# A second V row tile for the recurrent forward, and the next segment's tail rows issued behind the copies of V rows on GpSimd

## Chip, cores, metric

One core of one Trainium2 chip. The metric is device microseconds of a whole execution (forward and all gradients), median of the executions of one kernel. With one core there are no two dies to compare; all profiled runs below are marked fast (granted clock 0.961 to 0.982 over the span).

## The reference, cut to what matters

The program computes a conditioned transformer block and its gradients. The change touches the forward of part A, a recurrence over 64 segments of 32 rows, with 8 memory rows handed on from each segment to the next (32 heads of 128):

```python
mem = mem0
for s in range(n_seg):                     # 64
    h = concatenate([mem, x[:, s*32:(s+1)*32]], axis=1)   # 40 rows
    q, k, v = h @ Wq, h @ Wk, h @ Wv
    p = softmax(where(mask, q @ k.T * scale, -1e9))
    o = (p @ v) @ Wo
    mem = o[:, :8]                          # the next segment needs these
    outs.append(o[:, 8:])
```

## The kernel before

Rows of a segment are split. The first 32 of its 40 rows (8 memory rows and 24 of x) are projected in the segment itself. The last 8 ("tail rows") of four segments are projected together ahead of time into RB. `Vst` holds V by head: rows 0 to 95 are copied from `RA["v"]` on GpSimd (`Vst<-RA0v`), the tail rows 96 to 119 come by six small transfers from `RBv`, issued by GpSimd (`v_tails`). Two transposing transfers on the SyncE queue write V and the exponentials transposed (`VTr<-Vst`, `Pst<-ET`) for the backward. GpSimd scales `Pst` in the next segment (`norm`).

```python
Vst = ptiles("Vst", 1)[0]                       # one tile
...
def v_tails(s):
    rb, o = RBv[(s // nseg_t) % 2], 8 * (s % nseg_t)
    for j in range(3):
        nc.gpsimd.dma_start(Vst[96 + 8*j:104 + 8*j, 0:1024], rb[32*j + o:32*j + o + 8, 0:1024])
        nc.gpsimd.dma_start(Vst[96 + 8*j:104 + 8*j, 1024:1408], rb[96 + o:104 + o, 384*j:384*j + 384])
...
for s in range(NS):                             # one segment
    if norms: norms.pop()()                     # scaling of Pst of segment s-1, then its stores (SyncE)
    proj("k", 0, "dve"); proj("k", 1, "act")    # K rows; half 1 also issues the row store
    if 1 <= s4 <= 3:                            # s4 = s % 4
        p1(s // nseg_t + P1_AHEAD, s4)          # a layernorm step on VectorE: statistics, scale, shift
    proj("q", 0, "dve"); proj("q", 1, "act")
    proj("v", 0, "dve")
    nc.gpsimd.tensor_copy(Vst[0:96, 0:512], RA["v"][0:96, 0:512])       # L776
    turns()                                     # K and Q to heads
    proj("v", 1, "dve")
    nc.gpsimd.tensor_copy(Vst[0:96, 512:1024], RA["v"][0:96, 512:1024]) # L779
    st_exp(0); st_exp(1); vshift(); st_exp(2)
    nc.sync.dma_start(VTr[:], Vst[:, :], transpose=True)                # L793
    den(0); or0 = pv(0)                         # L733: product with Vst
    nc.sync.dma_start(Pst[:], ET[:, :], transpose=True)                 # L798
    ...                                         # pv(1), pv(2), Ost, OT
    at_ps = outproj()
    evac_turned()
    v_tails(s + 1)                              # overwrites Vst: waits for L793's transfer
    tails_in("kq", s + 1)                       # K and Q tails, eight GpSimd copies
    parts = self.split_pair(sb2, at_ps, "at")
    tail.collect(s4, [OT])
    ...                                         # memory rows to the next segment's hT
    self.store_rows(psp, sb2, ft, self.AOA[s], "at", "p")
    if s4 == nseg_t - 1:
        tail.begin(s - nseg_t + 1, [Wo])
    def norm(...):
        nc.gpsimd.tensor_tensor(Pst[0:120], Pst[0:120], rden..., op=mult)   # L851, 2.53 us
        nc.sync.dma_start(self.VT[s], VTr[:])
        nc.sync.dma_start(self.PS[s], Pst[:])                               # L854
    norms.append(norm)
```

All instructions are pinned to program order within their engine. So an instruction that waits holds up everything behind it on that engine: in the segment shown in the prediction L653 waited 4.12 us, to 873.22, and the copies of K and Q tails, which stand behind the six issues and do not need the transpose, started at 876.24.

The softmax here doesn't subtract the row's maximum and nothing guards it: scores larger than these inputs give would overflow.

## Time and profile before

| | before |
|---|---|
| time, median | 3292.5 us (3288.9 to 3294.4, 4 runs) |
| profiled span | 3281.5 us (a run of 3283.3 us, not one of these four) |
| forward: first K product of segment 0 to that of segment 63 | 34.1 to 1083.6 us |
| mean segment (62, the first left out) | 16.45 us |
| TensorE idle in 50 to 1100 us | 89 us |
| windows of 3.41 us at half clock, 100 to 1000 us | 20 |

The lines behind this stand in the prediction. Three things to read from them: which idle time of TensorE is large, what GpSimd does right before that wait ends, and what the next transpose on the SyncE queue had to wait for. The half-clock windows (stretches in which TensorE was granted 0.5 of its clock) are counted from the trace's records of the granted clock, their total time divided by 3.41 us, the length of the shortest of them there.

### The profile page before, as it was taken

What the parts mean: (1) busy time and instruction counts of PE and PEld (TensorE: products, weight loads), DVE (VectorE), ACT (ScalarE), POOL (GpSimd) and SP (SyncE); (2) the same over time, 40 slices, a digit from 0 to 9 for tenths busy, and PEclk for the clock granted to TensorE, in tenths of its full rate; (3) what the DMA queues carried; (4) which work ended last, traced back from release to release, by engine and by line L of the source; (5) the groups of instructions that cost most, each with busy time, mean ns of one, the idle gap of its engine ahead of it and who ended that gap; (6) DMA issues with size and microseconds to landing.
All of it is one profiled execution on the core that took longest, in us unless ns stands there. A gap on an engine that the chain in (4) does not pass through costs nothing.

```text
span 3281.5 us, 98764 instructions
## 1 busy us (share of the span) xinstructions
PE 3020.3 (92%) x40069; PEld 1756.2 (54%) x40069; DVE 1550.0 (47%) x3769; ACT 1160.6 (35%) x2829; POOL 1478.0 (45%) x2973
## 2 busy tenths in 40 slices
PE   5999998999899799997989999999999978999999
PEld 3565655656565444444545555555555543455454
DVE  4555555555555577753235455455555530332321
ACT  2444444444444333322124444444444420110111
POOL 3566665566555366641134444444444430332321
PEclk8999999999999799999999999999999999999999
DMA  8777877777777689887669999999999999998886
GB/s 291 186 186 188 194 190 178 194 187 191 181 185 186 206 208 220 217 231 244 223 169 273 259 259 262 265 262 266 272 263 259 263 235 218 247 213 191 199 231 159
DMA packets 958892, 726.12 MB, mean 221 GB/s; under 512 B 656018, under 2 KB 831138, under 8 KB 958308
## 3 DMA queue, kind: packets, MB, share of 16 engines
q1 hardware_dynamic: 827940, 508.77, 67.9%
q0 software_dynamic: 59056, 148.62, 13.4%
q10 hardware_dynamic: 71440, 62.40, 7.5%
q8 instruction: 316, 5.18, 0.7%
q14 instruction: 140, 1.15, 0.1%
HBM read 294.91 MB, written 276.33 MB: 174 GB/s over the span
## 4 chain that ended last, share of the span: by engine, by line
PE 39%; DMA 8%; issue 5%; ACT 2%; POOL 1%; DVE 1%; SPq 1%; ACTq 0%; POOLq 0%; DVEq 0%
PE dh_ps L212 9%; PE gps L1812 5%; PE pass_ps L249 4%; PE g_ps L1501 3%; PE gps5o L1825 3%; PE gps L1210 3%; PE dh_tps L212 2%; DMA rows<-DKR 2%; PE tps L1416 2%; DMA rows<-OSR 1%; PE dp_ps L1480 1%; PE dp_ps L1488 1%; ACT RAd L61 1%; PE dh_ft L318 1%; PE turn_ps L1382 1%
## 5 line engine op out<-in xcount | busy, mean ns | idle before, releaser
L1812 PE MATMUL gps<-rows,hrows 128*128 128x512 bf16 (+2 forms) x2160 | 417.6, 355 | 1.7 <-ACT ot L61 1.7
L1812 PEld LDWEIGHTS <-hrows 128*128 128x128 bf16 x2160 | 211.3, 98 | 206.3 <-issue 2.1
L249 PEld LDWEIGHTS <-hT 128*32 128x32 bf16 x6144 | 158.0, 97 | 161.4 <-issue 1.8
L1530 POOL COPY dOst<-RAd 96x512 bf16<-96x512 bf16 x128 | 78.5, 614 | 349.5 <-DVE RAd L63 339.4
L653 POOL DMA_DIRECT2D Vst<-RBv x192 | 97.8, 509 | 210.9 <-PE pass_ps L249 122.9
L1816 POOL DMA_DIRECT2D out_dram<-ot x108 | 81.5, 755 | 238.4 <-DVE ot L63 134.3
L63 DVE CAST ot<-gps 128x512 bf16<-128x512 f32 (+3 forms) x76 | 47.9, 633 | 259.2 <-PE gps L1812 142.8
L309 DVE TENSOR_TENSOR dh_lo<-dh_ps,dh_hi 128x256 bf16<-128x256 f32 x128 | 48.4, 420 | 239.1 <-ACT dh_hi L305 239.1
L851 POOL TENSOR_TENSOR Pst<-Pst,rden 120x1408 bf16<-120x1408 bf16 x63 | 159.4, 2530 | 0.0
L1825 PE MATMUL gps5o<-WoT,rows 128*128 128x512 bf16 x600 | 133.2, 384 | 24.1 <-DMA rows<-OSR 24.1
L61 ACT ACTIVATE ot<-gps 128x512 bf16<-128x512 f32 (+3 forms) x75 | 41.1, 548 | 291.8 <-PE gps L1812 139.0
L220 PE MATMUL at_ps<-Wo,OT 128*32 128x256 bf16 x4096 | 138.7, 294 | 0.4
L212 PE MATMUL dh_ps<-WvT,dVT 128*32 128x512 bf16 x2048 | 134.0, 380 | 0.0
L249 PE MATMUL pass_ps<-Wv,hT 128*32 128x512 bf16 x2048 | 133.3, 380 | 0.0
L63 DVE CAST RA0v<-pass_ps 128x512 bf16<-128x512 f32 x128 | 88.5, 692 | 88.9 <-PE pass_ps L249 62.0
L733 PE MATMUL or_ps<-Vst,ET 128*128 128x128 bf16 x704 | 71.7, 228 | 62.9 <-POOL Vst L776 56.6
L1490 DVE SCALAR_TENSOR_TENSOR dS<-dp_ps,Pst_l 128x512 bf16<-128x512 f32 (+1 forms) x192 | 112.2, 640 | 36.6 <-PE dp_ps L1488 36.5
L249 PE MATMUL pass_ps<-WoT,dyT 128*32 128x512 bf16 x2048 | 121.9, 380 | 5.2 <-ACT dyT L1589 5.2
L249 PE MATMUL pass_ps<-Wk,hT 128*32 128x512 bf16 x2048 | 122.8, 382 | 1.5 <-ACT hT L841 1.1
L212 PE MATMUL dh_ps<-WqT,dQT 128*32 128x512 bf16 x2048 | 122.3, 379 | 0.0
L212 PE MATMUL dh_ps<-WkT,dKT 128*32 128x512 bf16 x2048 | 122.3, 380 | 0.0
L61 ACT ACTIVATE dVT<-g_ps 128x512 bf16<-128x512 f32 (+1 forms) x192 | 107.8, 561 | 40.6 <-PE g_ps L1501 22.3
(407 smaller groups left out, 7104.7 us busy)
## 6 DMA issues: line engine op xcount, KB each, us to landing
OSR<-Ost SPq DMA_DIRECT2D x64, 352.0 KB
OT<-OT SPq DMA_DIRECT2D x64, 352.0 KB
VT<-VTr SPq DMA_DIRECT2D x64, 352.0 KB
PS<-Pst SPq DMA_DIRECT2D x64, 352.0 KB
OT_l<-OT SPq DMA_DIRECT2D x64, 352.0 KB
Pst_l<-PS SPq DMA_DIRECT2D x64, 352.0 KB
VT_l<-VT SPq DMA_DIRECT2D x64, 352.0 KB
DKR<-rows_x POOLq DMA_DIRECT2D x64, 352.0 KB, 5.8
```

The costliest lines, as they stand in the source:

```text
L61: return nc.scalar.activation(out, in_, AF.Copy)
L63: return nc.vector.tensor_copy(out, in_)
L212: self.nc.tensor.matmul(ps[32 * j:32 * j + 32, :], lhsT=lhsT, rhs=w, start=(n < 4), stop=(n >= total - 4), tile_position=(0, 32 * j))
L220: nc.tensor.matmul(ps[32 * j:32 * j + 32, :], lhsT=x[k], rhs=w[k][:, 256 * d:256 * d + 256], start=(n == 0), stop=(n == total - 1), tile_p ...
L249: self.nc.tensor.matmul(ps[32 * j:32 * j + 32, :], lhsT=lhs(c), rhs=rhs, start=(c == 0), stop=(c == DC - 1), tile_position=(0, 32 * j))
L653: nc.gpsimd.dma_start(Vst[96 + 8 * j:104 + 8 * j, 0:1024], rb[32 * j + o:32 * j + o + 8, 0:1024])
L851: nc.gpsimd.tensor_tensor(Pst[0:120, :, :], Pst[0:120, :, :], rden[:, :].unsqueeze(2).to_broadcast([120, G, 128]), op=ALU.mult)
L1210: nc.tensor.matmul(ps[:], lhsT=h2r[:, j, c * 128:(c + 1) * 128], rhs=xr[:, j, :], start=(j == 0), stop=(j == NT - 1))
L1490: nc.vector.scalar_tensor_tensor(out=part3(dS, pi), in0=ps[:, 0:n, :], scalar=cfg.scale, in1=part3(Pst, pi), op0=ALU.mult, op1=ALU.mult)
L1501: nc.tensor.matmul(ps[:, j, :], lhsT=lh[:, g * GW:(g + 1) * GW], rhs=rh[:, g * GW:(g + 1) * GW], start=True, stop=True)
L1812: nc.tensor.matmul(ps[:, 0:ng * E], lhsT=hrows[:, tp_, c * 128:(c + 1) * 128], rhs=rows[:, tp_, 0:ng * E], start=(tp_ == 0), stop=(tp_ == ...
L1825: nc.tensor.matmul(pss[gg][:], lhsT=rows[:, tp_, gg * E:(gg + 1) * E], rhs=dyrows[:, tp_, :], start=(tp_ == order[0]), stop=(tp_ == order[ ...
```

## The change

The intent: the tail rows of the next segment go into the other of two V tiles, so they need not wait for the transpose of the present one; and they are issued where GpSimd has nothing to do.

```diff
-            Vst = ptiles("Vst", 1)[0]
+            Vsts = ptiles("Vst", 2)
@@ def v_tails(s)
-                rb, o = RBv[(s // nseg_t) % 2], 8 * (s % nseg_t)
+                Vst, rb, o = Vsts[s % 2], RBv[(s // nseg_t) % 2], 8 * (s % nseg_t)
@@ for s in range(NS)
-                QT, KT = XT["q"], XT["k"]
+                QT, KT, Vst = XT["q"], XT["k"], Vsts[s % 2]
@@ behind the copies L776, L779
                     v_tails(0)
+                if s + 1 < NS:
+                    v_tails(s + 1)
@@ behind outproj(), evac_turned()
                 if s + 1 < NS:
-                    v_tails(s + 1)
                     tails_in("kq", s + 1)
```

## The prediction

> **What bounds the kernel now.** I read, in this order: the page's busy shares, a table of busy time by stretch, the list of waits in the forward stretch (50 to 1100 us), the timelines of TensorE, GpSimd and the SyncE queue over some segments, and the granted clock of single segments. The forward runs 64 segments one after the other, each needing the 8 memory rows of the one before.
>
> The stretch table says that TensorE is busy for 961 of the forward's 1050 us, so all its idle time there is 89 us. Columns: length, then busy us of TensorE, its weight loads, VectorE, ScalarE, GpSimd, then granted clock and DMA share.
>
> ```profile
> 50.00:1100.00 1050.00, 961.08 (x17827) 625.23 (x17828) 557.91 (x1482) 471.11 (x1277) 627.82 (x1341) 0.96 0.75 186
> ```
>
> The waits of that stretch (waiter, what ended the wait, us in total, times, longest):
>
> ```profile
> POOL Vst L653 <- PE pass_ps L249: 122.9, 34, 10.6
> ...
> PE or_ps L733 <- POOL Vst L776: 56.6, 43, 2.8
> ...
> POOL Vst L653 <- DMA VTr<-Vst: 53.9, 18, 4.5
> ...
> PE st_ps L690 <- POOL qT L65: 7.0, 4, 2.3
> ```
>
> Two thirds of TensorE's idle time are one wait: the first product with V (or_ps, L733) waits for GpSimd's copy of V rows into Vst (L776) in 43 of 64 segments. GpSimd in turn sits idle ahead of the tail-row issues (L653), 3.3 us a segment (210.9 us over 64). Most of these waits are put down to a TensorE product long done; the instruction's other wait is the transposing DMA that reads Vst, and I take it to be that one nearly everywhere. One stalled segment on GpSimd, as its timeline has it:
>
> ```profile
> 873.22 0.53 POOL L653 DMA_DIRECT2D Vst<-RBv  x1 [4.12 <-PE pass_ps L249]
> ...
> 875.74 0.51 POOL L654 DMA_DIRECT2D Vst<-RBv  x1
> 876.24 0.76 POOL L65 COPY kT<-b_colsk 128x192 bf16<-128x192 bf16 x4
> 876.95 0.77 POOL L65 COPY qT<-b_colsq 128x192 bf16<-128x192 bf16 x4
> 877.67 0.40 POOL L1886 COPY ao_tail<-OT 128x264 bf16<-128x264 bf16 x1
> 878.02 0.26 POOL L539 COPY hT<-hx 128x96 bf16<-128x96 bf16 x1
> 878.25 2.53 POOL L851 TENSOR_TENSOR Pst<-Pst,rden 120x1408 bf16<-120x1408 bf16 x1
> 880.74 0.60 POOL L776 COPY Vst<-RA0v 96x512 bf16<-96x512 bf16 x1
> 881.29 0.60 POOL L779 COPY Vst<-RA0v 96x512 bf16<-96x512 bf16 x1
> ```
>
> and on the SyncE queue in the same time:
>
> ```profile
> 866.74 1.39 SPq L793 DMA_TRANSPOSE VTr<-Vst  x1
> 868.23 2.04 SPq L798 DMA_TRANSPOSE Pst<-ET  x1
> ...
> 880.81 0.33 SPq L854 DMA_DIRECT2D PS<-Pst  x1
> ...
> 883.60 1.53 SPq L793 DMA_TRANSPOSE VTr<-Vst  x1
> ```
>
> The reader should see a ring. The transpose of Vst is issued at 866.74. The tail rows overwrite the only Vst, so their issue waits for it until 873.22 (6.5 us). Six issues (3.0), eight copies of K and Q tails (1.4), two small copies (0.6) follow in program order, then the scaling of Pst at 878.25 (2.53). The V copy and the store of Pst come behind it (880.74, 880.81); four more issues of the same queue end and the next transpose leaves at 883.60. Round the ring: 16.86 us. From the traces' instruction times over all segments the usual round is 10.8 (transpose issue to scaling) + 2.5 + about 3.1 = 16.4 us. The forward's mean segment is 16.45 (62 segments after the first in 1020 us). So the ring paces most segments, not TensorE alone.
>
> What TensorE needs without stalls is in its timeline: the first Wk products of three consecutive segments start at 582.25, 597.14 and 611.89, so 14.89 and 14.75 us. Sixteen segments with extra conditioning products take 0.66 more.
>
> The stalls cost a second time, through the clock. Columns as above:
>
> ```profile
> 856.50:871.20 14.70, 14.36 (x280) 9.21 (x276) 9.09 (x25) 7.02 (x19) 9.54 (x21) 1.00 0.72 170
> 871.20:889.40 18.20, 16.10 (x291) 10.33 (x287) 9.45 (x24) 7.51 (x20) 9.27 (x20) 0.91 0.76 179
> ```
>
> The second is the segment shown, with 1.98 us of stall; its period is 3.5 us longer than the one before, and TensorE's own busy time is 1.7 us longer at a granted clock of 0.91. The clock records hold about 25 windows of 3.41 us at half clock between 121 and 1100 us.
>
> [...] 0.50 us in the timeline, 3.8 us median to landing for Vst<-RBv. So the six issues are 3.0 us of GpSimd's own time, and moving them doesn't shorten them. [...]
>
> **The change part by part.**
> Removed: the wait of the tail rows for the transpose of the same segment. They now write the other Vst, whose transpose was issued a whole segment earlier and lands around the start of this one; the new place, behind L779, is about 8 us into the segment. I expect no wait there.
> Added: one memset of 0.65 us at the start, and six issues more in segment 0; nothing per segment. The build order shows 2529 GpSimd rows both before and after.
> Moved: 3.0 us of issues, from between the transpose and the scaling to behind the V copies, where GpSimd sat idle for some 3 us until the memory rows (AOA) were ready. That hides them.
>
> The new ring: K and Q tails, collection and hT copy (2.0 us) no longer stand behind the transpose, and run right after AOA near the end of the segment. The scaling then waits for its own input only, the transposed Pst. That one leaves 1.6 us after Vst's. The queue's own waits give its landing where they were still open:
>
> ```profile
> SPq L854 <- DMA Pst<-ET: 12.9, 22, 0.9
> ```
>
> In the rows with a real wait these end 6.0 to 8.0 us after Vst's transpose was issued, usually 7.2. So the ring becomes 7.2 + 2.5 + 3.1 = 12.8 us, 3.6 less than now and about 1.9 below TensorE's 14.75. TensorE should then be the bound: with a transpose issued 9 us into a segment, Pst lands at 16.2, 1.4 into the next; scaling ends at 4.0, before the V rows arrive (5.4), and the V copies finish well ahead of the product at 8.0.
>
> The sum: 62 segments at 14.76 make 915 us, plus 16 x 0.66 = 11, so 926 against 1020: at most 94 us. About 64 of it are direct stalls (56.6 and 7.0); the rest is mostly half-clock time, 25 windows with up to 1.7 us lost in each, partly in the forward's first segments. Not all goes: I leave 8 us for late transposes where the queue also stores the tail K and Q rows (3.8 us of issues in half the segments), [...]and for a few half-clock windows. Gain 86 us, all from the forward; everything behind it is untouched. 3294 - 86 = 3208 us.
>
> **The rivals.**
> First: the landing of Pst takes the place of the removed wait and stays late. Scaling must stand ahead of the V copy in program order, so a late Pst stalls TensorE just as before. For it: [...]DMA share is already 0.75 and rises by a tenth when segments shorten. Against it: landing 6 to 8 us after issue leaves 1 to 2.7 us of slack. If it were true half of the time, the gain would be 40 to 55 us, time 3240 to 3254.
> Second: only the direct wait goes, the half-clock windows stay, since they also come in segments with small stalls. Then the gain is 60 us and the time 3234. Against it: the segments without stall that I checked run at 1.00.
> Third: the SyncE queue becomes the bound, as its stores of tail rows and the four row stores stand ahead of the next transpose. It would hold segments near 15.3 in half of the cases: gain some 75, time 3219.
> Fourth: nothing gained, because the six issues now delay AOA and the K and Q tails. These come at 12 us with two to three to spare, so I give this little.
>
> **Range and chances.** 2% is 3228, a gain of 66. The main line and the third rival are beyond it, the first two are not. I give 0.84 to faster, 0.14 to within 2%, 0.02 to slower; 8 in 10 between 3194 and 3242.
>
> **What would show it.** Right: the wait of or_ps for L776 falls from 56.6 to under 10 us; L653's idle time for the transpose is gone; GpSimd now shows idle time ahead of L851, put down to the transpose of Pst; the segment falls to about 14.9; half-clock windows in the forward fall from 25 to under 8; the forward's end moves from about 1105 to about 1020. Wrong: if or_ps still waits for L776 with L851 ending later than 6 us into the segment, the first rival holds; if the segment is 15.3 with L793 late and no L776 wait, the third; if the waits go and the clock stays at 0.96, the second.

## The result, and the profile after

| | before | after |
|---|---|---|
| time, median | 3292.5 us | 3201.2 us (3194.5 to 3208.4, 4 runs) |
| profiled span | 3281.5 us | 3198.9 us |
| forward, first to last K product | 1049.5 us | 967.4 us (33.8 to 1001.2) |
| mean segment | 16.45 us | 15.1 us |
| half-clock windows, 100 to 1000 us | 20 | 0 |

The ratio is 0.9724, 95% interval 0.9701 to 0.9748. Ratios here are the mean time of one kernel's fast runs over that of the other's of the same rounds, so not quite the ratio of the medians. The rest of the program, from the first K product of segment 63 to the end, varies by 24 us (2193 to 2217 us over the twelve profiled runs), so the length of the forward is the finer measure, and I use it below.

The stretch table, from the first K product of segment 0 to that of segment 63 and so with the same 17858 TensorE products in both, first before, then after (length, busy us of TensorE, weight loads, VectorE, ScalarE, GpSimd, granted clock, DMA share, GB/s):

```profile
34.10:1083.60 1049.50, 963.34 (x17858) 624.53 (x17858) 558.88 (x1482) 470.84 (x1274) 618.88 (x1329) 0.96 0.76 189
```

```profile
33.80:1001.20 967.40, 934.17 (x17858) 600.69 (x17858) 595.92 (x1482) 469.43 (x1274) 623.27 (x1335) 0.99 0.85 205
```

TensorE's idle time fell from 86 to 33 us, and its busy time by 29 us for the same work. That second part goes with the granted clock, 0.96 before and 0.99 now: the clock records hold 91.1 us at half clock in the first stretch and 10.7 in the second. VectorE's busy time rose by 37 us, which nothing in the diff explains; it comes back below.

The waits in the forward (50 to 1010 us) of the kernel after (lines of the file move by one):

```profile
POOL Pst L852 <- issue: 80.1, 39, 3.6
...
POOL Pst L852 <- DMA Pst<-ET: 24.0, 13, 4.9
...
PE turn_ps L258 <- DVE RA0q L63: 5.9, 9, 1.0
```

The wait of or_ps for L776 is not in the list any more: it was 56.6 us. GpSimd now waits ahead of the scaling, 104 us, in part put down to "issue", where the profile shows no releaser; in the two runs with added copies below, the same wait is put down to the landing of the transposed Pst. TensorE has a small new wait, for the Q rows that VectorE writes.

One segment on GpSimd after:

```profile
561.08 0.61 POOL L779 COPY Vst<-RA0v 96x512 bf16<-96x512 bf16 x1 [1.37 <-DVE RA0v L63]
561.63 0.57 POOL L653 DMA_DIRECT2D Vst<-RBv  x1
...
565.74 0.55 POOL L333 DMA_DIRECT2D AOA<-at_rb  x1
566.28 0.76 POOL L65 COPY kT<-b_colsk 128x192 bf16<-128x192 bf16 x4
...
568.04 0.26 POOL L539 COPY hT<-hx 128x96 bf16<-128x96 bf16 x1
569.87 2.54 POOL L852 TENSOR_TENSOR Pst<-Pst,rden 120x1408 bf16<-120x1408 bf16 x1 [1.57 <-issue]
574.68 0.61 POOL L776 COPY Vst<-RA0v 96x512 bf16<-96x512 bf16 x1 [2.27 <-DVE RA0v L63]
```

and the SyncE queue beside it:

```profile
562.09 1.43 SPq L795 DMA_TRANSPOSE VTr<-Vst  x1
...
573.73 0.37 SPq L855 DMA_DIRECT2D PS<-Pst  x1
...
577.56 1.45 SPq L795 DMA_TRANSPOSE VTr<-Vst  x1
```

The six issues follow L779 without a wait. The scaling starts 7.8 us after the transpose was issued (before: 11.5 in the segment shown in the prediction; medians over all 63: 7.7 and 10.8). And the V copy L776 now waits for its rows (2.27 us), so the scaling no longer sets it: the slack has gone from TensorE to GpSimd.

### The profile page after: what moved, and what is told of

Read it like the earlier page. It is cut to its first block, busy times and chain, and to the rows that moved or that the text cites.

```text
span 3198.9 us, 98797 instructions
## 1 busy us (share of the span) xinstructions
PE 2986.2 (93%) x39993; PEld 1731.2 (54%) x40069; DVE 1587.3 (50%) x3770; ACT 1158.8 (36%) x2829; POOL 1475.9 (46%) x2973
## 4 chain that ended last, share of the span: by engine, by line
PE 36%; DMA 11%; issue 5%; ACT 2%; DVE 2%; POOL 2%; SPq 1%; ACTq 0%; POOLq 0%; DVEq 0%
PE dh_ps L212 9%; PE pass_ps L249 4%; PE gps L1813 4%; PE g_ps L1502 4%; PE gps L1211 3%; PE dh_tps L212 2%; DMA rows<-DKR 2%; PE tps L1417 2%; PE dp_ps L1481 1%; PE gps5o L1826 1%; PE dp_ps L1489 1%; ACT RAd L61 1%; DMA rows<-OSR 1%; PE dh_ft L318 1%; DMA Kst<-KST 1%
## 5 line engine op out<-in xcount | busy, mean ns | idle before, releaser
L63 DVE CAST ot<-gps 128x512 bf16<-128x512 f32 (+3 forms) x76 | 47.9, 633 | 250.1 <-PE gps L1813 128.2
L220 PE MATMUL at_ps<-Wo,OT 128*32 128x256 bf16 x4096 | 125.1, 275 | 0.5 <-DVE OT L63 0.2
L249 PE MATMUL pass_ps<-Wq,hT 128*32 128x512 bf16 x2048 | 121.8, 379 | 0.0
L63 DVE CAST RA0v<-pass_ps 128x512 bf16<-128x512 f32 x128 | 88.3, 690 | 65.9 <-PE pass_ps L249 63.6
L694 ACT ACTIVATE ET<-st_ps 128x480 bf16<-128x480 f32 (+1 forms) x192 | 96.0, 535 | 54.2 <-ACT qT L61 37.3
```

Source lines behind the costliest of these rows:

```text
L63: return nc.vector.tensor_copy(out, in_)
L220: nc.tensor.matmul(ps[32 * j:32 * j + 32, :], lhsT=x[k], rhs=w[k][:, 256 * d:256 * d + 256], start=(n == 0), stop=(n == total - 1), tile_p ...
L249: self.nc.tensor.matmul(ps[32 * j:32 * j + 32, :], lhsT=lhs(c), rhs=rhs, start=(c == 0), stop=(c == DC - 1), tile_position=(0, 32 * j))
L694: nc.scalar.activation(part3(ET, pi)[:, 0:n, 0:120], st_ps[:, 0:n, 0:120], AF.Exp, scale=cfg.scale)
```

## The experiments

Ten runs. The theory: a ring through GpSimd and the SyncE queue (transpose of Vst, tail issues, K and Q tails, scaling, store of Pst, row stores, next transpose) paced the segments at 16.4 us; the change cuts it to about 12.8, under what TensorE needs. The rivals: the gain is 3.0 us of GpSimd work moved into idle time; or only the wait on the tile counts; or the SyncE queue is no part of it. Each run's own expectation is quoted with it.

Overview, with the forward's length from the profiled run and the half-clock windows between 100 and 1000 us:

| run | time us | ratio to before (95%) | forward us | half-clock |
|---|---|---|---|---|
| e1_two_tiles_old_place | 3207.8 | 0.9762 (0.9726 to 0.9798) | 971.6 | 0 |
| e2_one_tile_tails_later | 3236.4 | 0.9855 (0.9804 to 0.9906) | 999.9 | 4 |
| e3_before_store_behind | 3221.2 | 0.9803 (0.9770 to 0.9837) | 986.5 | 6 |
| e6_after_6_copies | 3343.3 | 1.0174 (1.0139 to 1.0209) | 1108.4 | 34 |
| after_again | 3202.7 | 0.9747 (0.9718 to 0.9776) | 967.3 | 0 |
| e5_after_2_copies | 3203.3 | 0.9735 (0.9707 to 0.9763) | 963.8 | 0 |
| e4_after_ln_moved | 3185.9 | 0.9696 (0.9668 to 0.9724) | 956.6 | 0 |
| e7_before_ln_moved | 3290.8 | 1.0014 (0.9989 to 1.0039) | 1053.9 | 24 |
| e8_one_tile_both_moved | 3200.9 | 0.9743 (0.9719 to 0.9766) | 966.3 | 2 |
| e4_again | 3191.7 | 0.9698 (0.9681 to 0.9716) | 957.1 | 0 |

All gave correct results. The first four shared a chip job (before: 3284.2 us), so did the next four (3287.1) and the last two (3288.8).

### Which half of the change: the tile, or the place?

```diff
 # e1: the changed kernel, v_tails back at its old place
-                if s + 1 < NS:
-                    v_tails(s + 1)
                 if s == NS - 1:
@@
                 evac_turned()
                 if s + 1 < NS:
+                    v_tails(s + 1)
                     tails_in("kq", s + 1)
```

> Two V row tiles, but the six tail issues stay at their old place, behind AOA. Ring theory: the wait for the transpose of Vst is gone, so GpSimd runs AOA (ends 12.2 us into the segment), six issues to 15.2, K and Q tails, collection and hT to 17.3, which is 2.5 into the next segment; scaling then starts at 2.5 instead of the 0.4 to 2.5 of the changed kernel and ends at 5.1, still ahead of the V rows at 5.4. So nearly all of the gain: 3200 to 3215 us, segments of 14.9 to 15.2, the wait of or_ps for L776 under 5 us. Rival (the gain is the 3.0 us of issues moved into idle time of GpSimd): the place is what counts, so at most a third of the gain, 3260 or more.

Measured: 3207.8 us, forward 971.6 against 967.4. The scaling starts 2.8 us into the segment in the median (2.5 was worked out), and the L776 wait is 1.9 us in four segments. So the second tile alone gives nearly all of the gain, and the place adds some 4 us of forward. The rival of moved GpSimd work is out.

### Must the second tile be there at all?

```diff
 # e2: the kernel before, one tile, another order
                 if s + 1 < NS:
-                    v_tails(s + 1)
                     tails_in("kq", s + 1)
                 parts = self.split_pair(sb2, at_ps, "at")
                 tail.collect(s4, [OT])
+                if s + 1 < NS:
+                    v_tails(s + 1)
```

> The kernel before with one tile; only the order on GpSimd changes: the K and Q tails and the collection (1.8 us) go ahead of the V tail issues, so they pass while the transpose is under way. Ring theory: 16.4 less 1.8 is about 14.6 to 15, close to what TensorE needs, so most of the gain without a second tile: 3215 to 3245 us, segments of 15.0 to 15.6, the L776 wait 5 to 25 us. Rival (the write-after-read wait itself must go, a shorter ring does nothing as it is the transpose that sets the time): 3280 or more.

Measured: 3236.4 us, forward 999.9: in the range. With 1.8 us out of the ring, the L776 wait nearly went. The waits in the forward of this run:

```profile
PE turn_ps L258 <- DVE RA0q L63: 22.5, 12, 2.0
...
PE turn_ps L258 <- DVE RA1q L63: 9.3, 9, 1.1
...
PE or_ps L733 <- POOL Vst L776: 5.2, 2, 3.0
```

The write-after-read wait on the one tile (a write that must stand back until the old contents have been read) is still there: GpSimd idles 30.5 us in all ahead of L653, where it was 210.9, and this costs little once the ring has room for it. So it was the sum around the ring that counted, not the wait as such. The mean segment is 15.6 us, at the upper end of the range. What is new is the wait for Q rows, as in the changed kernel but larger; e8 below mends it, and gains 33.6 us of forward.

### Does the ring pass through the SyncE queue?

```diff
 # e3: the kernel before; the store of Pst goes behind the row stores
+            ps_stores = []
@@ for s in range(NS)
                 st_exp(2)
+                if ps_stores:
+                    ps_stores.pop()()
                 if s < NS - 1:
                     nc.sync.dma_start(VTr[:], Vst[:, :], transpose=True)
@@ norm
                     nc.sync.dma_start(self.VT[s], VTr[:])
-                    nc.sync.dma_start(self.PS[s], Pst[:])
+                    ps_stores.append(lambda: nc.sync.dma_start(self.PS[s], Pst[:]))
```

> The kernel before with one edit on the SyncE queue: the store of the scaled Pst is issued behind the four K and Q row stores, right ahead of the transpose of Vst, not ahead of them. GpSimd's order and the single tile stay. Ring theory: the leg from the end of scaling to the next transpose falls from 3.1 us to about 1.2 (then it is the V copies that are waited for), the ring to 14.5 to 15: 3210 to 3240 us. Rival (the ring doesn't go through the SyncE queue, TensorE waits for GpSimd's own load alone): no change, 3280 to 3295.

Measured: 3221.2 us, with no second tile and GpSimd's order untouched. The wait for the V copy (the lines of this file move by one) fell from 56.6 us to:

```profile
PE or_ps L734 <- POOL Vst L777: 16.8, 14, 2.9
```

One store moved behind four others on another queue gave 63 of the forward's 82 us. The store waits for the scaling, and the row stores and the transpose waited behind it although they need nothing from it. The leg from scaling to transpose fell less than worked out, from 3.1 to 2.4 us in the mean, and the mean segment is 15.4 us in place of 14.5 to 15.

### Put the time back into the ring

```diff
 # e5 (2 copies) and e6 (6 copies): the changed kernel
+            junk = pt.tile([128, 4, 128], BF16, name="junk")
@@ for s in range(NS)
                 def norm(s=s, Pst=Pst, rden=rden):
+                    for _ in range(2):      # e6: 6
+                        nc.gpsimd.tensor_copy(junk[0:96, 0:4, :], Pst[0:96, 0:4, :])
                     nc.gpsimd.tensor_tensor(Pst[0:120, :, :], ...
```

> The changed kernel with six useless GpSimd copies of 96x512 (0.6 us each, 3.6 in all) that read the transposed Pst ahead of the scaling, so that they lie in the ring and nowhere else is anything changed. Ring theory: 12.8 + 3.6 = 16.4 us again, so the gain goes: segments near 16.4, 3270 to 3300 us, or_ps waits for L776 again (40 to 70 us), and half-clock windows come back. Rival (the gain came from GpSimd's total load or from the wait on the tile alone): GpSimd is busy 9.8 us of 15, 3.6 more fit into its idle time, so 3200 to 3215.

> The changed kernel with two useless GpSimd copies (1.2 us) ahead of the scaling, as against six in the run before, which gave 3343 us. Ring theory: 12.8 + 1.2 = 14.0 us is still under TensorE's 14.75, so there is no stall for Vst: 0 to 15 us more than the changed kernel[...]. Rival (each us on GpSimd costs the same, whatever the ring): six copies cost 142 us, so two cost 47 us.

Two copies cost nothing: 3203.3 against 3202.7 us in the same rounds. Six cost 140 us. That is the mark of a ring with slack: free until it is used up. In e5 the slack is all but used: the scaling starts 8.95 us after the transpose (median), and with 2.5 and 3.1 that makes 14.6 us, by the same sum, against TensorE's 14.75. By my estimate two copies also push the scaling partly off VectorE's layernorm steps (the next section), so they give a little as well as take: TensorE's wait for RA0q is 3.7 us in place of 5.9, and e5's forward is 3.5 us shorter. Six were dearer than I expected (3270 to 3300). Its timelines tell why; GpSimd first (lines move by three), then the SyncE queue:

```profile
571.98 4.39 POOL L854 COPY junk<-Pst 96x512 bf16<-96x512 bf16 x6 [2.53 <-DMA Pst<-ET]
576.46 2.53 POOL L855 TENSOR_TENSOR Pst<-Pst,rden 120x1408 bf16<-120x1408 bf16 x1
```

```profile
564.25 2.07 SPq L796 DMA_TRANSPOSE VTr<-Vst  x1
...
581.78 1.58 SPq L796 DMA_TRANSPOSE VTr<-Vst  x1
```

Pst landed 7.7 us after the first issue, six copies took 4.4 in place of 3.6, the scaling 2.5, the stores 2.8: 17.5 us, while the mean segment is 17.4. The same timeline also gives the releaser that "issue" hid: here the wait ahead of the first reader of Pst is put down to the transpose. The wait list of e6 has the symptom of the kernel before again, and more of it (50 to 1130 us):

```profile
POOL junk L854 <- DMA Pst<-ET: 190.4, 62, 4.8
...
PE or_ps L734 <- POOL Vst L777: 93.2, 56, 3.0
```

With the stalls came 34 half-clock windows, from 0. So the clock's part of the gain comes and goes with these stalls.

### The wait that the change brought

VectorE's layernorm steps in the forward (min, median and max ns of one), first before, then after, then in e4:

```profile
L401 DVE TENSOR_SCALAR xh<-x,mv,rstd x14: 537/540/574, 82.5 to 939.4; 128x512 f32<-128x512 bf16 x14
...
L406 DVE TENSOR_TENSOR h<-xh,sa_bc x14: 681/682/684, 97.2 to 954.6; 128x512 bf16<-128x512 f32 x14
```

```profile
L401 DVE TENSOR_SCALAR xh<-x,mv,rstd x14: 537/1747/2836, 80.8 to 871.2; 128x512 f32<-128x512 bf16 x14
...
L406 DVE TENSOR_TENSOR h<-xh,sa_bc x14: 682/2335/2986, 96.5 to 885.9; 128x512 bf16<-128x512 f32 x14
```

```profile
L401 DVE TENSOR_SCALAR xh<-x,mv,rstd x14: 536/538/541, 78.8 to 858.9; 128x512 f32<-128x512 bf16 x14
...
L406 DVE TENSOR_TENSOR h<-xh,sa_bc x14: 681/682/1278, 93.5 to 873.6; 128x512 bf16<-128x512 f32 x14
```

The same instructions take three times as long after the change. In the segment shown above, VectorE's timeline has it beside GpSimd's scaling (569.87, 2.54 us):

```profile
570.18 2.51 DVE L401 TENSOR_SCALAR xh<-x,mv,rstd 128x512 f32<-128x512 bf16 x1
572.72 0.69 DVE L402 TENSOR_TENSOR xh<-xh,ca_bc 128x512 f32<-128x512 f32 x1
573.33 0.68 DVE L63 CAST RA0q<-pass_ps 128x512 bf16<-128x512 f32 x1
```

L401 ends with the scaling, 0.28 us later. The trace of the kernel after has the same all over (60 to 1000 us, 14 each of L401, L402 and L406): the 22 that started while the scaling ran, and one that started 0.02 us ahead of it, ended 0.28 or 0.29 us (L401) or 0.55 us (L402, L406) after the scaling did, and took up to 3.07 us. The 8 that started 0.03 to 0.58 us ahead of it kept their 0.54 to 0.69 us. VectorE's casts of product rows (L63) took no more time beside it: 80 of them ran with the scaling for over 0.3 us, and took 0.68 to 0.69. In e2 one L401 took 4.00 us (651.11 to 655.11), while GpSimd ran its last two tail issues (651.07 to 652.05), the hT copy and the scaling, which ended at 654.82. What holds the one kind back and not the other, no trace shows.

Before the change the scaling started 5.7 us into the segment in the median, when the layernorm step was done (none of the 42 met it); now it starts at 1.3.

```diff
 # e4: the changed kernel; e7: the same edit on the kernel before
-                if 1 <= s4 <= 3:
-                    p1(s // nseg_t + P1_AHEAD, s4)
                 proj("q", 0, "dve")
@@ end of the segment
                 if s4 == nseg_t - 1:
                     tail.begin(s - nseg_t + 1, [Wo])
+                else:
+                    p1(s // nseg_t + P1_AHEAD, s4 + 1)
```

> The changed kernel once more, as the one to compare with on this chip: 0.972 of the kernel before, within 0.003.

> The changed kernel with the three layernorm steps of VectorE (statistics, scaling, shift, one each in segments 1 to 3 of four) moved from between the K and Q projections to the end of the segment before. In the changed kernel these operations take 1.3 to 2.0 us in place of 0.55 to 0.7, as GpSimd's scaling of Pst runs at the same time, and TensorE waits 6 to 7 us for the Q rows behind them. Theory ([...]new with the change because scaling starts 3 to 4 us earlier in the segment): the operations fall to near 0.6 to 0.7 us, the waits for RA0q and RA1q go, the third and fourth segments of four fall from 15.3 and 15.1 to 14.7 to 14.9: 8 to 15 us less than the changed kernel. Rival (they are longer for another reason, or the waits are of the PSUM buffers): no difference, within 4 us.

> The same move of the layernorm steps in the kernel before, as a control: there the scaling runs 5 us or more into the segment, beside other work of VectorE, and the operations take 0.55 to 0.71 us. So nothing to gain: within 8 us of the kernel before. [...]

Measured: e4 gave 3185.9 us, the changed kernel beside it 3202.7; the forward fell from 967.3 to 956.6 us. The waits for RA0q and RA1q are gone, and the third and fourth of four segments fell from a mean of 15.3 and 15.1 to 14.9 and 14.9, and VectorE's busy time in the forward is back at 560 us. The control e7 is within 0.4% of the kernel before, so the move is worth nothing where the two operations do not meet. This version beats both kernels; its whole-time gain over the change (17 us by the medians) is less sure than the 10.7 us of the forward.

### The one-tile version with both orders mended

e2 and the edit of e4 together, on the kernel before:

> The kernel before with its one V row tile, with the V tail issues behind the K and Q tails and the collection (as in the run that gave 3236 us) and the layernorm steps moved to the end of the segment before (as in the run that gave 3186 us). Theory: with the ring near 14.6 us[...], TensorE is the bound and the second tile buys little: 3183 to 3200 us, segments of 14.7 to 14.9 in all four places. Rival (one tile keeps a wait that two do not have): 3205 or more, as the change itself.

> The changed kernel with the layernorm steps moved, once more beside the one-tile version on the same chip: 0.9696 of the kernel before, within 0.003.

Measured: 3200.9 us, just outside what was expected, and 9.2 us of forward behind e4_again. So one tile can do what the change does, but not all of what two do. Its GpSimd timeline shows where the rest went:

```profile
521.88 0.51 POOL L653 DMA_DIRECT2D Vst<-RBv  x1 [1.19 <-PE pass_ps L249]
525.32 0.52 POOL L654 DMA_DIRECT2D Vst<-RBv  x1 [2.93 <-PE pass_ps L249]
```

About every sixteenth segment GpSimd stands still for some 3 us in the middle of these issues. With one tile that falls into the ring, and the segments around it took 17.0, 18.5 and 18.3 us, where their neighbours take 15.4, 14.9 and 14.9. With two tiles it is nearly hidden: in the kernel after, the four segments with such a pause (2.66 to 2.81 us) took 16.1, 15.5, 14.7 and 14.2 us, those next to them 14.6 to 15.8. What causes the pauses is open; the TensorE product named was long done, and VectorE ran only two casts of 0.69 us from PSUM meanwhile. One thing the traces do show: in every run but e6 the pauses stand before the same ones of GpSimd's DMA issues, 121 issues apart, at whatever time these fall, and with two copies added (e5) as without. In the kernels before and after these are the issues 128, 249, 370 and 491 from the start, counted from 0: at 315.4, 564.9, 824.7 and 1089.3 us before (2.75 to 2.94 us), at 289.6, 520.7, 761.5 and 1000.1 us after. So in these runs they go with the count of issues.

## Why the prediction was right

**The time.** 3208 was predicted, 3201 measured, inside 3194 to 3242; a gain of 86 us, measured 91 by the medians here, 84 when both were run again, and 82 between the first and last K product of the forward. Of these 82, 53 are idle time of TensorE and 29 its busy time; the prediction had 64 of direct stalls, less what it left over, and the rest from the clock.

**What bounds the kernel now (the ring).** Right, and the experiments show each leg of it: e2 took out the K and Q tails, e3 the row stores, e1 the wait, e6 put 4.4 us back. Of these four edits of the same ring, each sized from its legs, three landed in the range worked out; e6 went past its range of 3270 to 3300 us, at 3343, as its copies and the landing of Pst took longer than counted.

**The part removed.** Right: L653 shows no wait for the transpose any more, and the L776 wait went from 56.6 us to none.

**The part moved.** "That hides them" is right, but e1 shows it to be worth only some 4 us of forward. The text gave no separate number for it; its sum let one think that both parts were needed.

**The new ring of 12.8 us.** Not seen directly, as TensorE now sets the pace, and taken too short: the scaling starts 7.7 us after the transpose in the median, where 7.2 was taken for the landing of Pst, so the same sum gives 13.3. That there was slack is shown by e5, where 1.2 us more cost nothing.

**The clock.** Right: 20 half-clock windows between 100 and 1000 us became 0, and TensorE's busy time fell by 29 us for the same work. The second rival, that they would stay, is out. The size of a stall alone does not decide it: e2 had nine stalls of 2.0 to 2.2 us and 4 windows. The clock records show what the windows went with. All changes of clock of a run lie on a fixed grid of 3.413 us. I added up TensorE's idle time in each stretch of this grid at full clock (as the profile models the ends of its products), 100 to 1000 us. In the kernel before, all 9 stretches with over 1.72 us of it were followed by half clock, none of the 216 with under 0.95 us, and 6 of the 18 between. Over all twelve traces these were 42 of 42, none of some 2900, and 33 of 117. In e2 the four stalls that half clock followed lay within one grid stretch each, the other five were split by an edge. In the kernel after, no stretch holds more than 1.11 us. These are counts; what sets the clock, and where between 0.95 and 1.72 us, they do not show.

**The 8 us left over.** Nearly right in size, wrong in cause. I left them for late transposes with the queue's tail stores, pauses of about 3 us on GpSimd and rest windows of half clock. The segments total 11 us over the floor of 926, and e4 removes 10.7 of them: it was VectorE's layernorm steps, which took longer beside the scaling (L401 1.75 us in the median, 0.54 before), as that starts 4.4 us earlier in the segment (medians). No view of the kernel before hinted at it, since the two never met there. One could have asked it: what stands on VectorE at the place where a GpSimd operation moves to?

**The rivals.** First: it came in part. Pst does land late and takes the place of the removed wait (GpSimd's 104 us ahead of the scaling), but this does not reach TensorE: the wait for L776 is gone, and e5 shows room for 1.2 us more. Third: some segments are indeed at 15.3 to 15.8, but because of VectorE, not the SyncE queue. Fourth: out, the K and Q tails are in time.

## What to carry to other kernels

When an engine at 90% waits for a small copy, follow the copy's engine back until you meet the copy again one round later, and add up the legs. If the sum is the period, any leg can be cut, and the cheapest here was in a queue in which stores and a transpose waited behind a late store that they need nothing from (one moved line, e3, gave 63 of the 82 us of forward). After the cut, look for operations that became longer: an engine freed to run earlier can meet work of another engine beside which that takes longer, as L401 did here beside the scaling (0.54 to 1.75 us in the median).
